# Gated MLP plus spectral filter on one core: h through DRAM as Strassen-Winograd factors, and the down projection in seven products summed in PSUM

## The chip, the cores and the metric

One core of a Trainium2 chip runs the whole kernel. The metric is device time in microseconds of one execution: 1478.47 us, the median of 3 runs (1477.56 to 1479.11). The profile shown below is one further execution, whose span from first to last instruction is 1478.0 us.

## The reference

The input x is 2048 rows of 576 numbers. xn is x with each row brought to mean 0 and variance 1. The output is the sum of x, a spectral filter of xn and a gated MLP of xn:

```python
xn = _layernorm(x, axis=-1)
# A: X = rfft2(xn);  X = X * (w_r + 1j * w_i);  y = irfft2(X)
# B: g = xn @ w_gate; u = xn @ w_up; h = sigmoid(g) * u; y = h @ w_down
return x + _A_ref(xn, A_w_r, A_w_i) + _B_ref(xn, B_w_gate, B_w_up, B_w_down)
```

w_gate and w_up are 576 x 4608, w_down is 4608 x 576, all in float32. F below is the inner width 4608, cut into NF = 36 blocks of 128.

## The kernel before

Each float32 factor is split into a rounded high part (ACT copies it into fp32r) and a low part (DVE subtracts), and a product is three partial products: high by high, high by low, low by high. A product of a 288-row inner dimension takes seven matmuls of 512 columns (`prod`, L554; the last of them holds the 32 rows left over in all three combinations).

The rows of x go in two halves of 1024 ("pairs", p = 0 and 1), each in two chunks of 512. For a half, `X` holds seven transposed and split combinations of its four blocks A11, A12, A21, A22 (two chunks by two halves of D): the left factors of Strassen-Winograd's seven products. `fill` (L343) makes one by transposes on PE, with `prep` and `sums` ahead of it. For each block f of F, `make_w` (L217) loads gate and up columns (`load_raw`, L197) and makes the seven right factors; they go to DRAM (`wsp`, L231) in the first half and come back from there in the second (`get_w`, L243). `unit` (L585) then makes the seven products of one f for one half, 49 matmuls in all, and from their PSUM banks A, B and E the block of h: gate goes through the sigmoid, is multiplied with up (L638), and h is split into hh and hl (L640, L641). The first two blocks of F in each half (`plain`, L566) are done without Strassen-Winograd, with 28 matmuls for each block and chunk.

The down projection is plain. `down` (L643) multiplies, for one tile of 128 rows, two blocks of h (as stationary operand) by two blocks of w_down, split by `make_d` (L250), in two column halves of 288: 12 matmuls into a pair of PSUM banks. DVE then adds the 128 x 576 result to the tile's accumulator in SBUF (L659), which starts as x itself. This follows every second f, for eight tiles, and is issued within the next two units, behind their products 4 and 5.

The spectral part goes in three phases over 16 tiles each, `phase1b` (transform along D and the first stage along S, to DRAM `sc1`), `phase2` (second stage, filter, inverse of that stage, `sc1` to `sc2`), and `phase3` (rest of the inverse, added into the accumulator). Each phase is a generator; the second half of the program steps all active ones once after each product (`beside`, `aside`), and a table with base and rate (L41, L678) says at which step a tile begins. The constants of a phase are loaded in `stage1`, `stage2` and `stage3`. The accumulators of the first half go to DRAM (`spill`) and come back in `phase3`.

Nearly all DMAs are issued by SP's queue. The framework orders the instructions of an engine by its own planning, close to program order; only the first tiles are in an order written by hand (L706). On the chip each engine works in order.

## Time and profile before

| | |
|---|---|
| median of 3 runs | 1478.47 us |
| span of the profiled execution | 1478.0 us |
| PE busy | 1447.0 us, 8232 matmuls and transposes |
| DVE busy | 932.3 us |
| ACT busy | 596.4 us |
| DMA | 307.87 MB, mean 208 GB/s |
| last matmul begun and its chain | PE ends at 1472.7 us, then one add of 0.75 us and the output's DMA |

In the rows of a view, `out<-in` names tiles, x with a number is a count, and the first two numbers behind the bar are the group's busy time in us and the mean of one instruction in ns; behind the second bar stands the idle time just ahead of these instructions, with what ended it. In the rows of time stretches, each engine has its busy us and its count, followed by the granted TensorE clock, the busy share of the 16 DMA engines and GB/s. KB is 1024 bytes, GB/s counts 10^9.

### The profile page before, as it was taken

Reading aid. Unit: us, or ns where it says so; the run is one execution under the profiler, and the core shown is the slowest. Engines: PE = TensorE matmul, PEld = TensorE weight load, DVE = VectorE, ACT = ScalarE, POOL = GpSimd, SP = SyncE. Lnnn points to the kernel's source line nnn. Section 1 sums busy time; section 2 is a strip of 40 time slices with the busy share of each in tenths; the row PEclk is TensorE's granted clock in tenths of the full one; section 3 lists DMA queues with packets and bytes.
Section 4 is the critical chain, followed back from the end, with each engine's and each line's share of the span. In section 5 each row is a group of like instructions: output and inputs, shape, how many; then the busy total and the mean of one; then the engine's idle time right before and its main releaser. Section 6 shows DMA issues by size and latency. Waiting matters only on the chain.

```text
span 1478.0 us, 21446 instructions
## 1 busy us (share of the span) xinstructions
PE 1447.0 (98%) x8232; PEld 1274.7 (86%) x8232; DVE 932.3 (63%) x1608; ACT 596.4 (40%) x1023; POOL 9.7 (1%) x29
## 2 busy tenths in 40 slices
PE   4999999999999999999999999999999999999998
PEld 3788888888888888888888888888888898898897
DVE  4889777777777777766455555546666644555544
ACT  4734434344444434453334344334444433333331
POOL 2000000000000000000000000000000000000000
PEclk9999999999999999999999999999999999999999
DMA  7577666666666666665856455567777576654532
GB/s 210 191 238 244 223 239 239 232 228 225 227 219 216 223 232 238 230 203 195 270 172 212 159 189 170 174 208 243 235 242 247 181 255 223 224 161 163 179 110 65
DMA packets 150487, 307.87 MB, mean 208 GB/s; under 512 B 14064, under 2 KB 77808, under 8 KB 145520
## 3 DMA queue, kind: packets, MB, share of 16 engines
q1 hardware_dynamic: 149072, 304.00, 61.5%
q0 software_dynamic: 384, 1.18, 0.4%
q8 instruction: 65, 1.06, 0.3%
q10 hardware_dynamic: 928, 1.31, 0.2%
q14 instruction: 38, 0.31, 0.1%
HBM read 188.01 MB, written 118.42 MB: 207 GB/s over the span
## 4 chain that ended last, share of the span: by engine, by line
PE 91%; DMA 3%; DVE 3%; ACT 1%; SPq 1%; issue 1%; DVEq 0%; ACTq 0%; POOL 0%; POOLq 0%
PE po L654 30%; PE pB L554 21%; PE pE L554 16%; PE pA L554 15%; PE pe L511 2%; PE pd L401 2%; PE pa L412 1%; PE pc L456 1%; PE py L482 1%; PE pb L440 1%; DMA std<-in_B_w_down 1%; DMA acc<-in_A_x 1%; DMA x<-sc 0%; PE pf L386 0%; PE pz L494 0%
## 5 line engine op out<-in xcount | busy, mean ns | idle before, releaser
L654 PE MATMUL po<-wd,hh 128*128 128x288 f32 x2304 | 401.6, 296 | 2.5 <-DVE acc L659 1.6
L554 PE MATMUL pB<-X,w 128*128 128x512 f32 x1484 | 383.5, 394 | 4.1 <-ACT w L210 3.8
L659 DVE TENSOR_TENSOR acc<-acc,po 128x576 f32<-128x576 f32 x288 | 216.0, 752 | 236.6 <-PE po L654 235.1
L654 PEld LDWEIGHTS po<-wd,hh 128*128 128x128 f32 x2304 | 343.8, 188 | 16.9 <-DVE acc L659 3.6
L554 PEld LDWEIGHTS pB<-X,w 128*128 128x128 f32 x1484 | 271.9, 189 | 55.8 <-ACT w L210 4.2
L554 PE MATMUL pE<-X,w 128*128 128x512 f32 x1064 | 273.5, 392 | 0.0
L554 PE MATMUL pA<-X,w 128*128 128x512 f32 x1008 | 261.2, 394 | 0.6 <-DVE X L356 0.5
L654 PE MATMUL po<-wd,hl 128*128 128x288 f32 x1152 | 246.3, 295 | 0.0
L554 PEld LDWEIGHTS pE<-X,w 128*128 128x128 f32 x1064 | 193.1, 188 | 34.5
L554 PEld LDWEIGHTS pA<-X,w 128*128 128x128 f32 x1008 | 188.2, 190 | 38.1 <-DVE X L356 1.1
L654 PEld LDWEIGHTS po<-wd,hl 128*128 128x128 f32 x1152 | 186.3, 189 | 0.0
L210 ACT ACTIVATE w<-raw 128x768 fp32r<-128x768 f32 (+1 forms) x106 | 100.3, 947 | 108.2 <-PE pE L554 94.6
L618 ACT ACTIVATE g<-pB 128x512 f32<-128x512 f32 x68 | 40.6, 598 | 190.2 <-PE pB L554 190.2
L641 DVE TENSOR_TENSOR hl<-y,hh 128x1024 fp32r<-128x1024 f32 x67 | 82.1, 1225 | 30.0 <-ACT hh L640 29.0
L638 DVE TENSOR_TENSOR y<-y,g 128x1024 f32<-128x1024 f32 x67 | 82.0, 1224 | 3.4
L212 DVE TENSOR_TENSOR w<-raw,w 128x512 fp32r<-128x512 f32 (+1 forms) x106 | 81.9, 772 | 2.6 <-ACT w L210 2.2
L640 ACT ACTIVATE hh<-y 128x1024 fp32r<-128x1024 f32 x67 | 70.7, 1055 | 6.6 <-DVE y L638 6.2
L601 ACT ACTIVATE pB<-pA 128x512 f32<-128x512 f32 x68 | 39.6, 582 | 75.1 <-PE pA L554 75.1
L608 ACT ACTIVATE v<-pB 128x512 f32<-128x512 f32 x68 | 40.6, 597 | 66.0 <-PE pB L554 65.8
L615 DVE TENSOR_TENSOR y<-v,pE 128x512 f32<-128x512 f32 x68 | 46.6, 685 | 32.7 <-ACT v L614 31.6
L637 DVE TENSOR_TENSOR y<-v,pE 128x512 f32<-128x512 f32 x67 | 45.9, 686 | 26.6 <-PE pE L554 26.5
L183 DVE TENSOR_TENSOR al<-pd,ah 64x290 fp32r<-64x290 f32 x64 | 29.3, 458 | 41.0 <-ACT ah L182 40.5
(148 smaller groups left out, 1261.2 us busy)
## 6 DMA issues: line engine op xcount, KB each, us to landing
w<-wsp SPq DMA_DIRECT2D x246, 320.0 KB
wsp<-w SPq DMA_DIRECT2D x34, 2240.0 KB
wdsp<-wd SPq DMA_DIRECT2D x36, 576.0 KB
wd<-wdsp SPq DMA_DIRECT2D x36, 576.0 KB
std<-in_B_w_down SPq DMA_DIRECT2D x36, 288.0 KB
raw<-in_B_w_gate SPq DMA_DIRECT2D x72, 128.0 KB
raw<-in_B_w_up SPq DMA_DIRECT2D x72, 128.0 KB
sc<-x SPq DMA_DIRECT2D x16, 290.0 KB
```

The source lines that it names most:

```text
L210: nc.scalar.activation(o[:, :, :3, :], src, AF.Copy)
L212: nc.vector.tensor_tensor(o[:, :, 3:, :], src[:, :, :KT, :], f32(o[:, :, :KT, :]), op=OP.subtract)
L554: nc.tensor.matmul(bank, w[:, sw, :], X[:, x, sx, :], start=start and j == 0, stop=stop and j == len(STEPS) - 1, skip_group_check=skip)
L608: nc.scalar.activation(v[:, 0], bank["B"], AF.Copy)
L615: nc.vector.tensor_tensor(y[:, 1], v[:, 1], bank["E"], op=OP.add)
L618: nc.scalar.activation(g[:, 1], bank["B"], AF.Sigmoid)
L637: nc.vector.tensor_tensor(y[:, 0], v[:, 0], bank["E"], op=OP.add)
L638: nc.vector.tensor_tensor(y, y, g, op=OP.mult)
L640: ends.extend([first, lambda: nc.scalar.activation(hh, y, AF.Copy), lambda: nc.vector.tensor_tensor(hl, y, f32(hh), op=OP.subtract)])
L641: lambda: nc.vector.tensor_tensor(hl, y, f32(hh), op=OP.subtract)])
L654: nc.tensor.matmul(pd[:, b, :HD], l[:, c, cols], w[:, k, b * HD:(b + 1) * HD], start=g == 0 and l is hh and k == 0, stop=g == G - 1 and l ...
L659: nc.vector.tensor_tensor(a, a, pd[:, :, :HD], op=OP.add)
```

## The change

The program is parted in two. **Part one** makes all of h. X for all 2048 rows (seven factors for each half, in `xps`) stays on chip, so each f's right factors are made once and used for both halves: there is no `wsp` any more. The eight `plain` calls come first, then the units in the order (2,0), (3,0), (2,1), (3,1), then f by f with both halves. A unit's first product is issued inside the unit before (`ahead`). h stays in float32; for each pair of blocks, `export` makes the seven left factors of a second Strassen-Winograd and writes them to DRAM (`ssp`), and `make_t` does the same for w_down with split right factors (`tsp`).

**Part two** computes h times w_down: for each of seven products j and each half p, 18 steps k sum over all of F in four PSUM banks, one for each of four row tiles. A step loads a 128 x 512 block of the left factor (`fetch`), four steps ahead, splits it (`cut`), two steps ahead, and issues 12 matmuls of 288 columns. At k = 17 each bank is added to the accumulators by `evac`. All spectral phases move to part two, with one step of the generators at each of the 252 steps; the accumulators (16 tiles, each loaded from x in one of the first 16 steps) all stay on chip.

Core of the diff (`load_raw`, `make_w`, `fill` and the phases keep their instructions but for names and pools):

```diff
-U1, U2, U3 = (0, 4.1), (72, 4.1), (145, 4.7)
+NPR = NF // 2
...
+    def unit(u, beside, after):
+        f, p = u
+        h = new_h(f, p)
+        g = run.tile([P, 2, CW], F32, tag="g", name=f"g{f}_{p}")
+        B[u, "B"] = bank("bB", f"pB{f}_{p}")
+        B[u, "E"] = bank("bE", f"pE{f}_{p}", 2)
+        bA, bB, bE = (B[u, k] for k in "ABE")
+        nc.scalar.activation(bB, bA, AF.Copy)
+        made(u, "E", "P5", True)
+        beside()
+        made(u, "B", "P6", False)
+        nc.scalar.activation(h[:, 0], bB, AF.Copy)
+        beside()
+        made(u, "A", "P2", False)
+        nc.scalar.activation(g[:, 0], bA, AF.Sigmoid)
+        beside()
+        made(u, "B", "P7", False)
+        nc.scalar.activation(h[:, 1], bB, AF.Copy)
+        nc.vector.tensor_tensor(h[:, 1], h[:, 1], bE, op=OP.add)
+        beside()
+        if after:
+            ahead(after)
+        beside()
+        made(u, "B", "P4", False)
+        nc.scalar.activation(g[:, 1], bB, AF.Sigmoid)
+        beside()
+        made(u, "E", "P3", False)
+        nc.vector.tensor_tensor(h[:, 0], h[:, 0], bE, op=OP.add)
+        nc.vector.tensor_tensor(h, h, g, op=OP.mult)
+        beside()
...
+    def export(k, p):
+        a, b = H[2 * k, p], H[2 * k + 1, p]
+        A11, A21, A12, A22 = a[:, 0], a[:, 1], b[:, 0], b[:, 1]
+        def put(what, src):
+            nc.sync.dma_start(ssp[ORDER.index(what)][p][k], src)
+        put("P1", A11)
+        put("P2", A12)
+        put("P4", A22)
...
+        nc.vector.tensor_tensor(S1, A21, A22, op=OP.add)
+        put("P5", S1)
+        yield
+        nc.vector.tensor_tensor(S2, S1, A11, op=OP.subtract)
+        put("P6", S2)
+        yield
+        nc.vector.tensor_tensor(A21, A11, A21, op=OP.subtract)
+        put("P7", A21)
+        yield
+        nc.vector.tensor_tensor(S4, A12, S2, op=OP.subtract)
+        put("P3", S4)
...
+    ORDER = ("P1", "P2", "P6", "P7", "P4", "P5", "P3")
...
+        elif f >= 3 and p == (1 if f == 3 else 0) and f + 1 < NF:
+            make = make_w(f + 1)
...
+        elif p == 1 and f >= 4 and f + 2 < NF:
+            load_raw(f + 2)
+        if p == 1:
+            sides += [make_t(k) for k in range(NPR) if 4 + k * 5 // 3 == f]
+    finish(*sides)
+    one.close()
+    two = ExitStack()
...
+    def evac(what, p, m, b):
+        v = b[:, :HD]
...
+        if what == "P1":
+            U[p, m] = u = accp.tile([P, HD], F32, name=f"u{p}{m}")
+            nc.scalar.activation(u, v, AF.Copy)
+            add(c11, u)
+        elif what == "P2":
+            add(c11, v)
+        elif what == "P6":
+            add(U[p, m], v)
+            add(c12, U[p, m])
+        elif what == "P7":
+            add(U[p, m], v)
+            add(c21, U[p, m])
+            add(c22, U[p, m])
...
+    seq = [(j, p, k) for j in range(7) for p in range(HALVES) for k in range(NPR)]
+    def fetch(n):
...
+        if p == 0:
+            TT[j, k] = t = ring.tile([P, 2, HD], F32R, tag="t", name=f"tt{j}_{k}", bufs=NPR + 2)
+            nc.sync.dma_start(f32(t).rearrange("p a d -> p (a d)"), tsp[j][k])
+        SF[n] = s = ring.tile([P, CW], F32, tag="sf", name=f"sf{n}", bufs=4)
+        nc.sync.dma_start(s, ssp[j][p][k])
+    def cut(n):
...
+        SP_[n] = s = ring.tile([P, 2, CW], F32R, tag="sp", name=f"sp{n}", bufs=4)
+        split(s[:, 0], s[:, 1], SF[n])
...
+    for (base, rate), phase, n in (((2, 4.5), phase1b, HALVES * TPH), ((80, 4.5), phase2, N2 // 2), ((157, 4.8), phase3, HALVES * TPH)):
+        for t in range(n):
+            begin.setdefault(base + int(t * rate), []).append(lambda t=t, phase=phase: phase(t))
...
+    for n, (j, p, k) in enumerate(seq):
+        if n < HALVES * TPH:
+            load_x(acc[n], n)
+        fetch(n + 4)
+        cut(n + 2)
+        s, t = SP_.pop(n), TT[j, k]
+        for m in range(TPC):
+            if k == 0:
+                M[m] = ps.tile([P, CW], F32, tag=f"m{m}", name=f"m{j}_{p}{m}")
+            o = M[m][:, :HD]
+            for i, (a, b) in enumerate(((0, 0), (0, 1), (1, 0))):
+                nc.tensor.matmul(o, s[:, a, m * P:(m + 1) * P], t[:, b, :], start=k == 0 and i == 0, stop=k == NPR - 1 and i == 2)
+            if k == NPR - 1:
+                evac(ORDER[j], p, m, M[m])
+        active.extend(b() for b in begin.pop(n, []))
+        aside()
-    def down(p, j, m):
...
-            for l, k in ((hh, 0), (hh, 1), (hl, 0)):
-                for b in range(2):
-                    nc.tensor.matmul(pd[:, b, :HD], l[:, c, cols], w[:, k, b * HD:(b + 1) * HD],
-                                     start=g == 0 and l is hh and k == 0, stop=g == G - 1 and l is hl)
```

More of the change, by code (lines that the diff above doesn't have):

```diff
@@ L228, in make_w @@
         yield
[L229 to L232 removed]
+        yield from parts(new_w(f, 2, 2), raw[:, 1:3])
     def make_p(f):
         raw = RAW[f]
[L237 to L240 removed]
@@ new lines, in spectral_glu_kernel, with made, ahead @@
+    B = {}
+    def made(u, b, k, start, stop=True):
+        f, p = u
+        ka, kb = FACTORS[k]
+        prod(B[u, b], weight(f, kb), get_x(p, ka), start, stop, not start)
+    def ahead(u):
+        B[u, "A"] = bank("bA", f"pA{u[0]}_{u[1]}", 2)
+        made(u, "A", "P1", True)
+    def unit(u, beside, after):
+        f, p = u
+        h = new_h(f, p)
[25 more added lines that the diff above has]
+        nc.vector.tensor_tensor(h, h, g, op=OP.mult)
+        beside()
@@ new lines, in spectral_glu_kernel @@
+    ORDER = ("P1", "P2", "P6", "P7", "P4", "P5", "P3")
+    nc.vector.memset(rstd[:, :1], 1.0)
+    nc.scalar.dma_start(idf, con["id"])
+    nc.scalar.dma_start(f32(idr), con["id"])
+    nc.scalar.activation(nmr[:, :1], rstd[:, :1], AF.Sqrt)
+    stage_x(0, 0)
+    load_raw(0)
+    stage_x(0, 1)
+    load_raw(1)
+    stage_x(1, 0)
+    stage_x(1, 1)
+    b0 = bank("bB", "b0")
+    for i in range(CW // P):
+        nc.tensor.matmul(b0[:, i * P:(i + 1) * P], idr, idr, start=i == 0, stop=i == CW // P - 1, skip_group_check=True)
@@ new lines, in spectral_glu_kernel, with tick, finish @@
+    sides = []
+    def tick():
+        sides[:] = [g for g in sides if next(g, sides) is not sides]
+    def finish(*gs):
+        for g in gs:
+            for _ in g:
+                pass
+    queue = {0: [lambda: chunk(0, 1)], 1: [lambda: chunk_stats(1, 0)], 2: [lambda: chunk(1, 0), lambda: chunk_stats(1, 1)],
+             4: [lambda: chunk(1, 1), lambda: export(0, 0)], 5: [lambda: factors(0)]}
+    calls = [(f, p, c) for p in range(HALVES) for c in range(2) for f in range(2)]
+    for n, (f, p, c) in enumerate(calls):
+        sides += [q() for q in queue.get(n, [])]
+        if n == 1:
+            load_raw(2)
+            load_raw(3)
+        plain(f, p, c, tick)
+        if n in (0, 2, 4):
+            finish(*sides)
+            sides.clear()
@@ L364, in phase1b, with landed @@
+    pending = {}
+    def landed(t):
+        pending[t] -= 1
+        if pending[t] == 0:
+            for i, r in enumerate(rows(out, t)):
+                (nc.sync, nc.scalar)[i].dma_start(r, acc[t][i * N1:(i + 1) * N1, :])
     def phase1b(t):
@@ L518, in phase3 @@
         nc.vector.tensor_tensor(up, up, pe[:, 0, 1:HD], op=OP.add)
-        if t < TPP:
-            for i, r in enumerate(rows(out, t)):
-                nc.sync.dma_start(r, a[i * N1:(i + 1) * N1, :])
+        landed(t)
     def stage1():
```

697 lines of the change are left out of this document (296 added, 401 removed).

## The prediction

> **What bounds the kernel now.** I read the page first, for which engine fills the span and what the work is made of, then the chain that ended last.
>
> ```profile
> span 1478.0 us, 21446 instructions
> PE 1447.0 (98%) x8232; PEld 1274.7 (86%) x8232; DVE 932.3 (63%) x1608; ACT 596.4 (40%) x1023; POOL 9.7 (1%) x29
> PE 91%; DMA 3%; DVE 3%; ACT 1%; SPq 1%; issue 1%; DVEq 0%; ACTq 0%; POOL 0%; POOLq 0%
> L654 PE MATMUL po<-wd,hh 128*128 128x288 f32 x2304 | 401.6, 296 | 2.5 <-DVE acc L659 1.6
> L554 PE MATMUL pB<-X,w 128*128 128x512 f32 x1484 | 383.5, 394 | 4.1 <-ACT w L210 3.8
> L554 PE MATMUL pE<-X,w 128*128 128x512 f32 x1064 | 273.5, 392 | 0.0
> L554 PE MATMUL pA<-X,w 128*128 128x512 f32 x1008 | 261.2, 394 | 0.6 <-DVE X L356 0.5
> L654 PE MATMUL po<-wd,hl 128*128 128x288 f32 x1152 | 246.3, 295 | 0.0
> ```
>
> PE is the bound, and almost nothing is ahead of its matmuls. The work is 3556 products of 512 columns and 3456 of 288; the rest is the spectral part and transposes. The mean of one (296 ns) is a latency, since matmuls overlap. What one costs is its interval, from the chain and from PE's timeline:
>
> ```profile
> 304.94 3.18 PE po L654 x24
> 314.37 1.75 PE L554 MATMUL pA<-X,w 128*128 128x512 f32 x7
> 315.95 1.75 PE L554 MATMUL pE<-X,w 128*128 128x512 f32 x7
> ```
>
> 3.18 / 24 = 0.1325 us for 288 columns; seven of 512 take 315.95 - 314.37 = 1.58 us, 0.226 each. So 3556 x 0.226 = 804 us are gate and up, 3456 x 0.1325 = 458 us are down. Since the chain follows PE, a matmul removed is worth its interval as long as something feeds the others; the rest of this asks for that.
>
> **The change part by part.** *Matmuls.* Gate and up stay as they are: 8 plain calls of 28 and 68 units of 49 are again 3556. Down becomes 7 products x 2 halves x 18 steps x 4 tiles x 3 = 3024 instead of 3456. Each still has a stationary block of h and 288 moving columns, so the interval is kept: 432 x 0.1325 = **-57.2 us**. Without any other effect: 1478.0 - 57.2 = 1420.8. The profiled span is 0.5 us below the median of the runs, so I take it as the run's time.
>
> *Part one.* Without the 12-matmul blocks there are only products of 1.58 us, and the question is whether DVE keeps pace:
>
> ```profile
> 100.00:700.00 600.00, 599.02 (x3349) 531.85 (x3349) 447.33 (x742) 249.61 (x366) 0.00 (x0) 1.00 0.65 226
> L583 DVE TENSOR_TENSOR hl<-y,hh 128x512 fp32r<-128x512 f32 x6 | 4.1, 689 | 2.0 <-ACT hh L582 2.0
> L582 ACT ACTIVATE hh<-y 128x512 fp32r<-128x512 f32 x5 | 3.1, 629 | 4.7 <-DVE y L581 4.7
> L334 DVE TENSOR_TENSOR xa<-xa 128x288 f32<-128x288 f32 x4 | 1.6, 451 | 0.0
> ```
>
> DVE was 75% busy there, and PE had no hole. An f took 49 x 0.226 + 48 x 0.1325 = 17.4 us, so DVE spent 13.0 us on it. To that come, for an f of two units in 98 x 0.226 = 22.1 us: the second unit's adds (four times 128x512, 2.8 us), `export` (eight adds for two f, 2.8) and half of a `make_t` (eleven of 128x288, 2.5). That is 21.1 us even with nothing taken off for the accumulator adds and the split of h, which leave: it fits. I put part one's steady state at 0, hidden under PE; what it costs if a wait breaks that cover is the rival on late weights below.
>
> *The start.* It now prepares four chunks and both halves' factors beside plain calls and the first units; before, the second half's came later. Rows of PE's timeline, and the clock after the last hole:
>
> ```profile
> 12.72 0.69 PE L351 MATMUL px_A<-idf,xa 128*128 128x128 f32 x2 [7.35 <-ACT xa L329]
> 21.17 0.69 PE L351 MATMUL px_A<-idf,xa 128*128 128x128 f32 x2 [5.74 <-ACT xa L329]
> 37.64 1.70 PE L554 MATMUL pB<-X,w 128*128 128x512 f32 x3 [3.76 <-ACT w L210]
> 36.00:42.00 6.00, 3.88 (x14) 2.66 (x15) 5.24 (x20) 5.75 (x10) 0.00 (x0) 0.57 0.57 191
> ```
>
> The holes of 7.35, 5.74 and 3.76 us are waits on x and the first weights. w_down's load and split leave this place, but the second chunk's x now goes behind eight weight loads on SP instead of POOL. In those 6 us DVE is 5.24 busy: it sets the pace of preparing, and twice as much of it now lies under about 50 us of plain calls. Between -5 (w_down gone) and +12 (about two holes more), I take **+2**.
>
> *The seam.* Between the parts stands a DRAM round trip and memory handed from X to the new buffers. The nearest row is the one in the middle of the spectral part, on the chain:
>
> ```profile
> 968.63 4.34 DMA sc<-x
> 972.99 7.11 DMA x<-sc
> ```
>
> If the first step had to wait for its write and read, 4.34 + 7.11 = 11.5 us. But product P1's first pieces were written by the first export, hundreds of us earlier, and x0's buffers are free one unit (11 us) before the end; then it costs a fill of the pipe. After a hole of 3.76 us the clock was 0.57 for 6 us, 2.6 us lost, so 14 is the upper bound and 0 the lower. I take **+4**. The tail (PE's end, a DVE add, the output's DMA) is as before: 0.
>
> *Feeding part two.* This is the dear one. A step is 12 x 0.1325 = 1.59 us of PE, and in a first half (p = 0) it loads 256 KB of h's factor and 288 KB of w_down's. With that travel the spectral transfers:
>
> ```profile
> cf<-c_cf SPq DMA_DIRECT2D x1, 1450.0 KB
> acc<-in_A_x SPq DMA_DIRECT2D x24, 144.0 KB
> am<-c_am SPq DMA_DIRECT2D x16, 256.0 KB
> xb<-in_A_x SPq DMA_DIRECT2D x32, 144.0 KB
> x<-sc SPq DMA_DIRECT2D x16, 290.0 KB
> sc<-u SPq DMA_DIRECT2D x16, 290.0 KB
> wr<-in_A_w_r SPq DMA_DIRECT2D x32, 144.5 KB
> 805.00:810.00 5.00, 5.00 (x30) 4.24 (x28) 1.37 (x3) 2.48 (x7) 0.00 (x0) 1.00 1.03 405
> 850.00:855.00 5.00, 4.92 (x24) 3.78 (x24) 2.88 (x5) 2.85 (x6) 0.00 (x0) 1.00 1.00 364
> 325.00:330.00 5.00, 5.00 (x34) 4.70 (x34) 2.00 (x3) 0.60 (x1) 0.00 (x0) 1.00 1.01 420
> 1180.00:1200.00 20.00, 20.00 (x112) 17.71 (x112) 8.89 (x11) 6.34 (x10) 0.00 (x0) 1.00 0.87 308
> ```
>
> With the DMA engines full (share 1.00 to 1.03), 5 us moved 364, 405 and 420 GB/s. I take 380, between the first two, in which weights were read in rows of 2.5 KB, nearest to the new 2 and 2.3 KB. Where PE's own step is longer than its bytes, nothing is lost. Steps 0 to 15 also load an accumulator (2 x 144 KB): from step 2 with a tile of `phase1b` every 4.5 steps (256 + 288 + 290 KB; 20 matmuls of 290 columns and 6 transposes, about 3.1 us of PE), a step moves 1017 KB, 2.74 us, against 1.59 + 0.68 = 2.27 us: 14 x 0.47 = 6.6. Steps 0 and 1 lack the spectral cover and cf's 1450 KB go in step 1: 2 x 0.65 + 3.9 = 5.2. Steps 80 to 151 carry `phase2`: 290 + 4 x 144.5 + 290 KB for each tile (wr and wi, two loads each), 257 KB per step, against 12 matmuls, 0.35 us. In a first half that is 801 KB, 2.16 us, against 1.94; 36 steps of these are first halves: 7.8. The constants of `phase3`, as large as cf, fall into another: 3.9. Elsewhere PE's step is longer. Sum **+23 us**; the same sum gives 11 at 420, 29 at 364 and 66 at 308 GB/s.
>
> The Trainium skill ("DMA: Bandwidth & Descriptors", Specifications) puts HBM at about 358 GB/s for one core; by that the term would be 31 us. The rows at 405 and 420 GB/s lie above it, as the Trainium skill's "HBM Reference", Access, says of a core that streams alone.
>
> *Splitting h seven times* moves to part two: ACT 0.63 and DVE 0.69 us per step by the rows of L582 and L583, under 1.59 us of PE. With the spectral work DVE is the fuller one, in `phase2`:
>
> ```profile
> L183 DVE TENSOR_TENSOR x2l<-x,x2h 128x580 fp32r<-128x580 f32 x16 | 12.1, 755 | 3.3 <-ACT x2h L182 3.3
> L447 DVE TENSOR_TENSOR z<-wr,pb 128x512 f32<-128x512 f32 (+2 forms) x48 | 16.7, 352 | 20.6 <-ACT sw L443 16.9 <-DMA w<-wsp 3.4
> L449 DVE TENSOR_TENSOR z<-z,t 128x578 f32<-128x578 f32 x16 | 12.1, 753 | 0.0
> L412 PEld LDWEIGHTS pa<-ah,am 128*128 128x128 f32 x64 | 11.7, 188 | 7.4 <-ACT ah L182 6.5
> L456 PEld LDWEIGHTS pc<-zh,bmt 128*128 128x128 f32 x64 | 11.2, 188 | 5.5 <-ACT zh L182 5.3
> ```
>
> A tile of it has two splits of 0.755, an add of 0.753 and twice three multiplies of 0.352: 4.4 us per 4.5 steps. That is 0.98 + 0.69 = 1.67 us per step, under 1.94: DVE is at 86% and not last.
>
> *Ends of products.* Each tile has one bank, so the next product's first matmul on it waits for the add out of it; cover is nine matmuls, 1.2 us. With one 0.451 us add per tile (0.4 us of PE) it just holds. P6 queues two and P7 three adds per tile: the last of four banks is read after 3 x 0.9 + 0.45 = 3.2 and 3 x 1.35 + 0.45 = 4.5 us, where PE needs it 2.4 us after the first: 0.8 + 2.1, for two halves 5.8; a `cut` of 0.69 in front at each of 14 ends would make it 15.5. Bounds 0 and 16, I take **+5**.
>
> *Spectral chains.* Before, PE's weight loads waited 7.4 and 5.5 us for ACT at the two worst places. The chains keep their steps, now one per 1.59 us or more: 0, from -10 (hidden where the feed is slower anyway) to +13 (these two waits twice as long).
>
> Sum: 1478.0 - 57.2 + 2 + 4 + 23 + 5 = **1455 us**.
>
> **The rivals.** *The feed does not sustain its rate (slower).* 405 and 364 GB/s are five full us; the best 20 us quoted have 308, at a share of 0.87. In part two SP issues every load in order, and a store of `phase1b` or `phase2` that waits for ACT holds back the next `fetch`, which is ahead by only four steps (two before `cut`). If such holes hold the feed to 308, the term is 66 and the time 1478.0 - 57.2 + 11 + 66 = 1498. It decides from 46 us of feed on, about 328 GB/s. For it: at steps 2 to 15 PE's own pace of 2.27 us would ask for 459 GB/s, more than any row. Against it: other steps ask far less, and most of part two is not bound by the feed.
>
> *All hidden.* The scheduler runs loads early enough and start and seam cost nothing: 1421. For it: PE went without holes at 226 GB/s. Against it: the bytes of steps 0 to 15.
>
> *The lower row of reads holds throughout*: with full engines, but 364 GB/s, the feed is 29 us and the time 1461. The row at 364 and, over 20 us, 308 speak for it, 405 against. The Trainium skill's limit of HBM above is the rule for this case; by it the time is 1463.
>
> *Weights come late in part one (no change).* `make_w` for f + 2 starts in the very unit behind whose predecessor `load_raw` is issued; before, it had a whole unit between.
>
> ```profile
> 324.63 1.24 SPq L204 DMA_DIRECT2D raw<-in_B_w_gate  x1
> 333.46 0.55 SPq L205 DMA_DIRECT2D raw<-in_B_w_up  x1
> ```
>
> Its eight loads took 334.01 - 324.63 = 9.4 us to issue. ACT, waiting for them, would hold the copies out of bank B behind it, for which PE has 1.58 us of cover. If each odd f (16 of them behind seven writes of `export`) lost 1.4 us: 23 us, 1478.
>
> **How the numbers follow.** Forecast 0.45, all hidden 0.15, the lower row 0.10, late weights 0.08, slow feed 0.22. A measurement of this kernel tells 0.2%, 3 us, from no change, so the first three are faster (0.70), late weights the same (0.08), slow feed slower (0.22). The forecast alone spans 1436 to 1472: feed 11 to 29, seam and ends at their bounds. The range 1426 to 1494 takes in all but half of the hidden case and the worse half of the slow feed.
>
> **What would show it.** Right: 3024 matmuls of 288 columns at 0.1325 us between starts; part two begun about 855 us into the span (804 us of products and the start's holes and transposes); a DMA share near 1 in the first 50 us of part two and in first halves under `phase2`, with PE's idle there put down to the split or its load; short holes at the ends of P6 and P7. Wrong: holes in part one behind ACT's `w<-raw` (late weights), a DMA share well under 1 where PE waits (the queue, not the bytes), DVE over 95% in part two, or a clock under 1.00 in the rows of part two, which would add PE time that I have not counted.

## The result, and the profile after

The changed kernel takes **1522.43 us** (median of 4 runs, 1514.74 to 1524.78) against 1478.79 us for the kernel before in the same session: a ratio of 1.0289 (95% interval 1.0263 to 1.0314). It is slower by about 44 us. The forecast was 1455 us in a range of 1426 to 1494.

First the page of the changed kernel: its span, the busy time of the engines, the granted TensorE clock and the DMA share in 40 slices of 38 us, and the down projection's group.

```profile
span 1519.5 us, 22486 instructions
PE 1437.7 (95%) x7800; PEld 1242.0 (82%) x7800; DVE 971.3 (64%) x1808; ACT 702.7 (46%) x1292; POOL 1.7 (0%) x20
PEclk9999999999999999999999987999999999999999
DMA  7234445545545555455554379788888888895954
L904 PE MATMUL m<-tt,sp 128*128 128x288 f32 x3024 | 453.8, 302 | 32.4 <-ACT sp L135 27.3
```

The 432 matmuls are gone (7800 for 8232), as the diff says. PE's busy share fell from 98% to 95%. The last row shows one place: 32.4 us of idle time stand ahead of the new matmuls, 27.3 of them ended by the rounding copy of h's factors. The DMA row jumps from mostly 4 and 5 tenths to 7 and more at the 24th slice, where part two begins.

For the rest I measured the time from each matmul's start to the next one's, form by form. Below, an *interval* is the usual value of that, and a *loss* is what single ones take beyond it. By that measure part two begins at 888.8 us, not at 855, and four things changed.

| | forecast, us | in the profile, us |
|---|---|---|
| 508 products of seven matmuls, each 1.587 us before | 0 | 508 x 0.053 = 27 |
| losses in part one behind its first 60 us | 0 | 20 |
| losses in the first 60 us (29.6 before) | 31.6 | 18.6 |
| losses in part two (35.8 outside the start before, kept, plus 4 + 23 + 5) | 68 | 30 + 35 + 26 + 7 = 98 |

The four terms of the last row are, by place: the first 60 us of part two 30, up to 300 us of it 35, from there to 410 us (the filter phase) 26, the rest 7. The differences are +27, +20, -13 and +30: 64 us, and 1455 + 64 = 1519, where the span is 1519.5. So the sum closes, and the question is what stands behind each. (The 27 us are the change of the usual value times a count; what it costs in time is asked below.)

The first difference can be read from two neighbouring rows of PE's timeline, the second from a stretch of part one; columns as in the rows of the prediction.

```profile
330.85 1.79 PE L349 MATMUL pA<-X0A,w 128*128 128x512 f32 x7
332.48 1.79 PE L349 MATMUL pB<-X0S,w 128*128 128x512 f32 x7
```

```profile
100.00:700.00 600.00, 593.01 (x2542) 473.62 (x2541) 397.53 (x644) 258.31 (x441) 0.00 (x0) 1.00 0.52 176
```

Seven matmuls take 332.48 - 330.85 = 1.63 us where they took 1.58, at a granted clock of 1.00, so it isn't the clock. And PE, which had one hole of a microsecond in these 600 us, now lacks seven, although DVE is *less* busy than before (397.53 for 447.33 us) and ACT is at 43%. A busy share does not tell this; the waits do. These are ScalarE's longest, by line and releaser (us in total, times, longest), in part one:

```profile
ACT tP L452 <- DMA ts<-tP: 128.5, 88, 5.7
ACT g L405 <- PE pB L349: 102.8, 48, 2.9
ACT h L392 <- PE pB L349: 75.9, 50, 3.7
```

The second and third are harmless: ACT is early and waits for a product. The first is new. L452 makes the rounded part of one w_down factor; its tile has one buffer, so it waits until the store of the factor before has landed. What that does shows in the timeline:

```profile
736.74 0.41 SPq L455 DMA_DIRECT2D ts<-tP  x1
...
738.83 1.81 PE L349 MATMUL pA<-X1A,w 128*128 128x512 f32 x7
...
741.38 0.44 ACT L452 ACTIVATE tP<-wd 128x288 fp32r<-128x288 f32 x1 [5.70 <-DMA ts<-tP]
...
741.73 0.58 ACT L392 ACTIVATE h<-pB 128x512 f32<-128x512 f32 x1
...
742.36 3.19 PE L349 MATMUL pB<-X1S,w 128*128 128x512 f32 x7 [1.72 <-ACT h L392]
```

ACT stands still for 5.70 us on a copy that nobody needs soon. Behind it in its queue stands the copy of h out of bank B, which PE's next product on that bank needs (there is one such bank), and PE waits 1.72 us. This is the usual case: followed back one by one in the trace, PE's holes of part one that end with a copy of ACT's sum to 13.4 us, and 9.3 of them stand right behind a copy of L452 that had just waited for a landing. Another 1.5 us stand behind L452 waiting for something else, 1.8 us behind the weights' copies (L203) waiting for VectorE.

In part two the first 60 us are the worst: three stretches of 20 us.

```profile
900.00:920.00 20.00, 8.12 (x30) 6.92 (x30) 3.02 (x6) 2.23 (x6) 0.10 (x1) 0.50 1.03 256
920.00:940.00 20.00, 16.80 (x92) 14.94 (x93) 8.80 (x16) 7.42 (x17) 0.10 (x1) 0.84 1.01 265
940.00:960.00 20.00, 16.12 (x96) 14.21 (x95) 6.85 (x13) 6.21 (x14) 0.10 (x1) 0.90 1.00 276
```

The DMA engines are full (1.00 to 1.03), yet they move 256 to 276 GB/s and not the 364 to 420 of the full stretches before. So it is bytes, as I forecast, but at another rate. The order of the transfers adds to it:

```profile
898.77 3.00 SPq L145 DMA_DIRECT2D acc<-in_A_x  x4
...
901.25 3.25 PE L904 MATMUL m<-tt,sp 128*128 128x288 f32 x12 [3.98 <-ACT sp L135]
...
907.06 0.33 SPq L865 DMA_DIRECT2D sf<-ss  x1
...
909.81 1.17 SPq L145 DMA_DIRECT2D acc<-in_A_x  x2
...
913.79 0.63 ACT L135 ACTIVATE sp<-sf 128x512 fp32r<-128x512 f32 x1 [12.59 <-DMA sf<-ss]
...
914.47 3.49 PE L904 MATMUL m<-tt,sp 128*128 128x288 f32 x12 [9.97 <-ACT sp L135]
```

The accumulators' loads, wanted some 15 steps later, stand in front of the factor that PE wants now. PE idles 3.98 and 9.97 us, and the clock is 0.50 in the first of the three stretches (0.75 from 899 to 960 us, and 0.93 in the filter phase, from 1195 to 1300 us).

PE's waits in part two do not all belong to the feed:

```profile
PE m L904 <- ACT sp L135: 27.3, 14, 10.0
PE pa L691 <- DVE al L136: 5.8, 7, 1.7
PE pc L735 <- ACT zh L135: 3.6, 5, 1.2
PE m L904 <- DVE sp L136: 2.7, 4, 1.1
PE m L904 <- DVE u L827: 2.2, 1, 2.2
```

The first and the fourth row, 30.0 us, are waits for the split of h's factors. The waits inside the spectral chains (`pa`, `pc` and smaller groups of `pd`, `pf` and `pz`) sum to 16.3 us, most of them between 949 and 1189 us, where the split accounts for only 3.1 us. In the same view of the second half of the kernel before (from 739 us on), PE's waits of all kinds sum to 1.8 us. The last row is the end of a product. The rest of the 98 us is in no wait of this view: intervals that are longer than usual, those at the lower clock among them.

### The profile page after: what moved, and what is told of

It is laid out like the page before. It is cut to its first block, busy times and chain, and to the rows that moved or that the text cites. A ratio compares the mean times of both kernels' runs of the same rounds, so it can differ in the third digit from the quotient of the medians.

```text
span 1519.5 us, 22486 instructions
## 1 busy us (share of the span) xinstructions
PE 1437.7 (95%) x7800; PEld 1242.0 (82%) x7800; DVE 971.3 (64%) x1808; ACT 702.7 (46%) x1292; POOL 1.7 (0%) x20
## 5 line engine op out<-in xcount | busy, mean ns | idle before, releaser
L904 PE MATMUL m<-tt,sp 128*128 128x288 f32 x3024 | 453.8, 302 | 32.4 <-ACT sp L135 27.3
L904 PEld LDWEIGHTS m<-tt,sp 128*128 128x128 f32 x3024 | 424.6, 193 | 38.3 <-ACT sp L135 31.0
L136 DVE TENSOR_TENSOR sp<-sf,sp 128x512 fp32r<-128x512 f32 x252 | 172.3, 689 | 124.8 <-ACT sp L135 122.3
L135 ACT ACTIVATE sp<-sf 128x512 fp32r<-128x512 f32 x252 | 157.3, 629 | 144.1 <-PE m L904 71.5
L349 PE MATMUL pA<-X0A,w 128*128 128x512 f32 (+1 forms) x518 | 137.3, 402 | 2.2 <-DVE w L205 1.4
L349 PE MATMUL pA<-X1A,w 128*128 128x512 f32 (+1 forms) x518 | 133.0, 396 | 0.0
L349 PE MATMUL pB<-X1S,w 128*128 128x512 f32 (+1 forms) x476 | 124.0, 400 | 3.2 <-ACT h L392 3.2
L349 PE MATMUL pE<-X0S,w 128*128 128x512 f32 (+1 forms) x490 | 126.4, 397 | 0.0
L203 ACT ACTIVATE w<-raw 128x768 fp32r<-128x768 f32 (+2 forms) x108 | 100.2, 931 | 56.2 <-DVE raw L229 27.1
L349 PE MATMUL pE<-X1S,w 128*128 128x512 f32 (+1 forms) x490 | 125.9, 396 | 0.0
L349 PE MATMUL pB<-X0S,w 128*128 128x512 f32 (+1 forms) x476 | 122.7, 397 | 0.6 <-ACT h L392 0.5
L452 ACT ACTIVATE tP<-wd 128x288 fp32r<-128x288 f32 x126 | 55.9, 443 | 139.1 <-DMA ts<-tP 128.5
```

The lines of the kernel that those rows point to most:

```text
L135: nc.scalar.activation(hi, src, AF.Copy)
L136: nc.vector.tensor_tensor(lo, src, f32(hi), op=OP.subtract)
L203: nc.scalar.activation(o[:, :, :3, :], src, AF.Copy)
L349: nc.tensor.matmul(b, w[:n, sw, :], xx[:n, sx, :], start=start and j == 0, stop=stop and j == len(STEPS) - 1, skip_group_check=skip)
L452: nc.scalar.activation(t[:, 0], src, AF.Copy)
L904: nc.tensor.matmul(o, s[:, a, m * P:(m + 1) * P], t[:, b, :], start=k == 0 and i == 0, stop=k == NPR - 1 and i == 2)
```

## The experiments

Each time stands beside the kernel before on the same chip (1476.9 to 1477.6 us in these sessions); the changed kernel's ratio is 1.0289. Where intervals of two ratios overlap, I read only the trace, not the difference. When I planned the first runs my theory was that the lengthened interval came from the last step of each product, which uses 96 rows instead of 128, that the waits on the tP store made the holes of part one, and that part two lost to bytes; the rivals were a held SP queue and the place of the weights in memory.

### The matmuls' interval

**Last step on 128 rows** (e1), and **the kernel before with 96 rows** (e2):

```diff
-            n = KR if sx == KT else P
+            n = P            # the unused rows of X are set to zero
```

> The changed kernel with all seven steps of a gate/up product on 128 rows again (unused rows set to zero once). Theory of the narrow step: the 96-row matmul, new in this change, lengthens the interval of the 512-column matmuls from 227 to about 234 ns; undone, intervals return to 227 ns, part one ends about 25 us earlier and the time falls by about 25 us (1497). Rival (the longer interval comes from what part one does beside PE: other places in SBUF, other traffic): intervals stay at 232 to 235 ns and the time is unchanged within 4 us.

> The kernel before with one thing of the change: the last step of each product on 96 rows instead of 128. Theory of the narrow step: intervals of the 512-column matmuls go from 227 to about 234 ns and the time rises by about 25 us (1503). Rival: intervals stay at 227 ns, time within 4 us of 1478.

e1: 1512.79 us, ratio 1.0239 (1.0209 to 1.027); seven matmuls still took 1.638 us. e2: 1485.55 us, ratio 1.0054 (1.0039 to 1.0069); 1.613 us. In the kernel before the narrow step does cost something, 8 us where I expected 25, but putting it right in the changed one does not bring 1.587 back. There is a second cause. By the sizes of the tiles ahead of them, the changed kernel's weight tiles do not begin at a multiple of 128 bytes in a partition's memory (the first two lie 96 bytes past one); before, all did. No trace shows addresses; the runs that move the tiles have to tell.

**Weights moved to multiples of 128 bytes** (e8), and **the kernel before with them moved off by 32** (e9):

```diff
+    nc.gpsimd.memset(run.tile([P, 24], F32, name="pad"), 0.0)   # last in its pool
```

This is e8's edit. e9 puts a pad of 32 bytes ahead of the weight tiles of the kernel before, and one of 96 behind them.

> The changed kernel with one pad of 96 bytes at the end of part one's right pool, so that the stationary blocks of gate and up begin at multiples of 128 bytes in SBUF, as in the kernel before, and not 96 behind one. Theory of the shifted weights: this place, not the narrow step, makes the interval of the 512-column matmuls 234 instead of 227 ns; it returns to near 227 (231 where the narrow step shows), and the time falls by 17 to 25 us. Rival (something else in part one): the interval stays at 232 to 235 ns, time within 4 us of the changed kernel.

> The kernel before with a pad of 32 bytes ahead of its weight tiles and of 96 behind them, so that the stationary blocks of gate and up begin 32 bytes behind a multiple of 128; all else keeps its place modulo 128. Theory of the shifted weights: interval 234 ns instead of 227 in all products, time up by 20 to 25 us. Rival: interval 227 ns, time unchanged within 4 us.

e8: 1517.26 us, 1.0268 (1.0239 to 1.0297), so no gain in time; products 6 and 4 still took 1.640 us, the others 1.596 to 1.618. e9: 1486.84 us, 1.0063 (1.0046 to 1.0079); its timeline:

```profile
331.58 1.79 PE L554 MATMUL pE<-X,w 128*128 128x512 f32 x7
333.21 1.79 PE L554 MATMUL pA<-X,w 128*128 128x512 f32 x7
```

1.63 us, with nothing changed in the kernel before but the place of its weights. The time tells less than the interval: 0.045 us more for each of 508 products would be 23 us, and the kernel took 9.7 us longer. **Both edits together** (e14):

> The changed kernel with both edits at once: the last step of each product on 128 rows (unused rows zero), and the weights moved so that each begins at a multiple of 128 bytes. Each alone left the seven 512-column matmuls of a product at 1638 and 1617 to 1640 ns, against 1587 in the kernel before. Theory of two causes that hide one another: 1585 to 1592 ns for seven, median interval 227 ns, part two begins at 862 to 870 us, time 1494 to 1503 us. Rival (a third cause, such as which bank or which factor stands where): intervals stay at 231 ns or more, time 1510 us or more.

e14: 1514.15 us, 1.0263 (1.0227 to 1.03). Five of a unit's seven products take 1.587 to 1.593 us, products 6 and 4 take 1.621, and the median interval is 227 ns as before: the two causes hide one another. Products 6 and 4 are the two that read the third weight tile, `new_w(f, 2)`; product 7, on the same bank B but from the second tile, takes 1.587 us. So the bank is not what slows them. In the program the small tiles `st` and `rs` lie between the third weight tile and the others; e15 and e16 below move them elsewhere, and there all seven products are alike. That the pad left the third tile off a multiple of 128 is the reading that fits; no run moved this tile alone. But the time hardly moved. Part two begins at 882.7 us instead of 888.8, because the losses of part one rose from 20 to 38 us:

```profile
100.00:700.00 600.00, 587.51 (x2558) 474.07 (x2557) 400.11 (x648) 261.05 (x444) 1.04 (x2) 1.00 0.51 176
```

2558 matmuls in 600 us for 2542 before the edits, with 12.5 us idle for 7.0. PE was not what set the pace of part one. On time my expectation (1494 to 1503) missed, and the holes became the first question.

### The holes of part one

**The stores of the factors issued by GpSimd** (e3), to take SP's queue out of the wait:

```diff
-            nc.sync.dma_start(tsp[ORDER.index(what)][k], ...)
+            nc.gpsimd.dma_start(tsp[ORDER.index(what)][k], ...)
```

> The changed kernel with the stores of w_down's factors in part one issued by POOL instead of SP. ACT waited 128 us in sum for the landing of the one buffer's store before it could fill it again, with the copies out of bank B behind it. Theory (these waits make part one's holes, some 17 us): the waits shrink by more than half, as the store no longer queues behind SP's weight loads, and the time falls by 8 to 15 us. Rival (the wait is the landing itself, not SP's queue, or the holes have another cause): ACT's waits stay above 100 us and the time changes by less than 4 us.

1562.2 us, 1.0586 (1.0564 to 1.0609): wrong in sign. The stores landed later (among those that a copy waited for, a median of 3.8 us behind VectorE's rest, for 2.8), and the wait grew from 128.5 us to this:

```profile
ACT tP L452 <- DMA ts<-tP: 209.0, 86, 5.5
```

The losses of part one went from 20 to 66 us, and 43 us of PE's holes now stand right behind such a wait, for 9.3. A longer wait on this line costs PE time; that much is shown.

**The factor's two parts in two tiles** (e10):

```diff
-            t = run.tile([P, 2, HD], F32R, tag="tt", ...)
+            hi = run.tile([P, HD], F32R, tag="th", ...)   # own store, one step earlier
+            lo = run.tile([P, HD], F32R, tag="tl", ...)
```

> The changed kernel, with the two parts of each w_down factor (its rounded value and its rest) in two tiles of one buffer each instead of one tile for both, each part written to DRAM on its own, the rounded value's store one step earlier. In the changed kernel ScalarE waited 128.5 us in 88 waits for the landing of the store before, with the copies of h queued behind it, and TensorE lost 20 us in the steady state of part one. Single-buffer theory (this wait costs TensorE the time): the waits fall to under 70 us, the holes to about 10 us, part two begins at 875 to 882 us instead of 888.8, time 1508 to 1515 us. Rival (the holes come from the length of ScalarE's and VectorE's own work, the wait only shows it): waits fall but the holes stay at 17 to 22 us, time 1519 to 1524 us.

1534.01 us, 1.0379 (1.0359 to 1.04), also the wrong way. The wait moved to another releaser and grew:

```profile
ACT thP L453 <- DVE tlP L457: 158.8, 76, 4.8
...
ACT thP L453 <- DMA ts<-thP: 43.2, 25, 5.4
```

The rounded part's buffer comes free only when VectorE has made the rest from it, and VectorE in its turn waits for the rest's buffer. Losses of part one: 30 us.

**Two buffers for the factor** (e15, on aligned weights), room made by writing one sum of `export` in place; and **with 128 rows too** (e16):

```diff
-            t = run.tile([P, 2, HD], F32R, tag="tt", name=f"t{what}{k}")
+            t = run.tile([P, 2, HD], F32R, tag="tt", name=f"t{what}{k}", bufs=2)
```

> The changed kernel with weights at multiples of 128 bytes (1617 to 1640 ns for seven matmuls, 1517.3 us measured before) and two buffers instead of one for the w_down factors of part one; the room comes from writing one sum of h's factors in place. It stands against that aligned kernel. Single-buffer theory: ScalarE's waits for the store's landing fall from over 100 us to under 20 us, the holes of part one's steady state from 29 to under 12 us, part two begins about 867 to 872 us instead of 887, time 1497 to 1504 us. Rival (ScalarE's and VectorE's own work sets the pace of part one): waits move to other lines, part two begins at 882 us or later, time 1512 us or more.

> As the run with two factor buffers, with the last step of each product on 128 rows as well. Without the two buffers these faster matmuls (1593 ns for seven on the banks A and E, 1620 to 1629 on B) raised the holes of part one from 20 to 38 us and moved its end by only 6 us. Single-buffer theory: holes under 15 us, part two begins at 846 to 856 us, time 1475 to 1487 us. Rival (ScalarE and VectorE set the pace): holes stay at 30 us or more, part two begins at 875 us or later, time 1505 us or more.

e15: 1521.73 us, 1.0295 (1.027 to 1.0319), with 1.613 us for seven matmuls, what e2's narrow step alone gave. e16: 1520.48 us, 1.0294 (1.0274 to 1.0315), although all seven-matmul products in it take 1.587 us, as before the change:

```profile
331.41 1.75 PE L351 MATMUL pE<-X0S,w 128*128 128x512 f32 x7
333.00 1.75 PE L351 MATMUL pB<-X0S,w 128*128 128x512 f32 x7
```

```profile
100.00:700.00 600.00, 576.88 (x2514) 464.70 (x2513) 409.94 (x680) 264.52 (x463) 1.04 (x2) 1.00 0.55 189
```

PE is idle for 23 of these 600 us. Waits for the landing stay at 93 us in 58 times in e15 and 99 us in 61 times in e16, the losses at 29 us (e15) and 39 us (e16), so a second buffer is no cure as the framework used it. But these runs are no clean test of the wait, since the order changed too: in e16 the copies come several in a row (a median of 2.3 us from one to the next, for 5.0 in e14), and the last is made at 603 us, for 828. Of the 30.6 us of e16's holes that end with a copy of ACT's, 19.6 us still stand right behind a wait for a landing. What the change of order shows by itself is more telling. These are two stretches of e16, the second behind the last of the copies:

```profile
300.00:500.00 200.00, 191.47 (x827) 153.28 (x825) 135.55 (x232) 88.29 (x158) 0.00 (x0) 1.00 0.59 203
700.00:860.00 160.00, 160.00 (x708) 132.53 (x707) 94.12 (x135) 60.96 (x93) 0.00 (x0) 1.00 0.32 113
```

PE lacks 8.5 us in the first and nothing in the second. The holes end with the work on w_down's factors.

**The factors' arithmetic taken out** (e19, on 128 rows and aligned weights): loads and stores stay, a constant tile is stored.

```diff
-            nc.scalar.activation(t[:, 0], src, AF.Copy)
-            nc.vector.tensor_tensor(t[:, 1], src, f32(t[:, 0]), op=OP.subtract)
-            nc.sync.dma_start(tsp[ORDER.index(what)][k], f32(t)...)
+            nc.sync.dma_start(tsp[ORDER.index(what)][k], f32(H["t"])...)   # H["t"] set once
```

> The changed kernel with aligned weights and 128-row last steps (1514.2 us, holes of part one 38 us, part two at 882.7 us), without the arithmetic on w_down's factors: ScalarE's 126 rounding copies and VectorE's 126 differences and its sums are left out, a constant tile is written to DRAM in their place, so loads and stores of w_down stay. Queue theory (these copies stand in ScalarE's queue ahead of the copies of h and g that TensorE's next product needs, and wait there for a store's landing): holes fall to under 10 us, part two begins at 848 to 856 us, time 1480 to 1488 us. Rival (the bank of the third sum, which has one buffer, makes the holes by itself): holes stay at 25 us or more, part two at 872 us or later, time 1503 us or more.

1489.78 us, 1.0083 (1.0062 to 1.0103). The losses of part one fall to 9.9 us, and part two begins at 855.2 us: the point that I had forecast.

```profile
100.00:700.00 600.00, 600.00 (x2650) 494.09 (x2649) 351.77 (x506) 231.86 (x357) 1.04 (x2) 1.00 0.52 178
```

PE has no hole in 600 us, with the same bank B and nearly the same bytes as e14 (178 GB/s for 176). More of them travel early: from 100 to 300 us it is 297 GB/s, and PE is busy for 200.00 of these 200 us. So the bank alone makes no holes, nor do the transfers; the factor work in the queues of ScalarE and VectorE does. That e14's and e19's medians lie 24 us apart is its price, in this version. Taking the wait and the work out one at a time would tell how they share it; e19 takes out both.

**All factor work on GpSimd** (e20, on e16, with two easings of part two):

```diff
-            nc.scalar.activation(t[:, 0], src, AF.Copy)
+            nc.gpsimd.tensor_copy(t[:, 0], src)
...
-            nc.vector.tensor_tensor(t[:, 1], src, f32(t[:, 0]), op=OP.subtract)
+            nc.gpsimd.tensor_tensor(t[:, 1], src, f32(t[:, 0]), op=OP.subtract)
```

> The changed kernel with aligned weights, 128-row last steps, two factor buffers, all work on w_down's factors (loads, copies, differences, stores) on GpSimd and its queue, and in part two factors fetched eight ahead and accumulators loaded every second step. Queue theory: part one's holes fall to under 12 us, part two begins at 850 to 858 us, its first 300 us lose 50 to 58 us instead of 65, time 1468 to 1480 us, about the kernel before. Rival (GpSimd is too slow for 126 pairs in part one, or takes VectorE's access to SBUF): holes of 25 us or more, or factors late for part two, time 1500 us or more.

1520.54 us, 1.0286 (1.0246 to 1.0326). The losses of part one stay at 38 us, with other releasers: PE's longest wait is now for VectorE (10.9 us), and ScalarE's copies still end 11.8 us of its waits. GpSimd's factor work is done at 535 us; from 700 to 860 us PE is busy throughout, as in e16. These are two of VectorE's groups from 100 to 500 us, first without GpSimd's work (e19), then with it (e20); the last pair of numbers before the second bar is busy us and mean ns.

```profile
L410 DVE TENSOR_TENSOR h<-h,pE 128x512 f32<-128x512 f32 x36 | 24.8, 688 | 87.6 <-PE pE L351 87.4
...
L431 DVE TENSOR_TENSOR s<-s,h 128x512 f32<-128x512 f32 x17 | 11.7, 689 | 0.3
```

```profile
L410 DVE TENSOR_TENSOR h<-h,pE 128x512 f32<-128x512 f32 x33 | 22.7, 688 | 57.6 <-PE pE L351 57.3
...
L431 DVE TENSOR_TENSOR s<-s,h 128x512 f32<-128x512 f32 x16 | 17.6, 1102 | 0.3
```

The add that takes one operand from PSUM keeps its 688 ns; the same add with both operands in SBUF goes from 689 to 1102 ns. So this moves the trouble to VectorE and settles nothing about a version with free queues on all sides, which I did not run.

### The feed of part two

**Stores and loads of the spectral phases on GpSimd's queue** (e4), for the rival that a held SP queue starves the factors:

```diff
-        nc.sync.dma_start(x2, ...)
+        nc.gpsimd.dma_start(x2, ...)     # also sc1, sc2 stores, w_r and w_i
```

> The changed kernel with four kinds of spectral transfers in part two (stores to sc1 and sc2, loads of x2 and of wr and wi) issued by POOL instead of SP; the bytes are the same. Theory of the held queue: SP, waiting for ACT's copy to store it, holds back the loads of h behind it; without that the 27 us that PE lost between 1200 and 1300 us fall below 10, time down 15 to 25 us. Theory of the bytes: the feed is short of GB/s, not of order; time changes by less than 5 us.

1516.68 us, 1.0266 (1.0249 to 1.0283), overlapping the changed kernel's interval. In the filter phase the losses fell from 26 to 20 us, from 60 to 300 us they rose from 35 to 44. What these four kinds of transfers hold up in SP's queue is not the main loss.

**Factors fetched eight steps ahead** (e5):

```diff
-        fetch(n + 4)
+        fetch(n + 8)     # sf bufs 4 to 8, t bufs NPR + 2 to NPR + 6
```

> The changed kernel with part two's loads issued eight steps ahead instead of four (eight buffers for h's blocks, four more for w_down's). Theory of the order (PE waits since SP is held by spectral stores or by a free buffer, while the DMA engines have room): PE's waits between 960 and 1300 us, some 50 us more than the products need, fall by more than half and the time by 20 to 35 us. Theory of the bytes (the engines are full there): they fall by less than a quarter, time down by under 8 us, and the first 60 us of part two stay as they are in both.

1511.01 us, 1.0224 (1.0208 to 1.024), about 10 us better by the ratios. The first 20 us of part two gained (93 matmuls and transposes for 30), the first 60 us as a whole lost 31 as before: depth shifts the bytes there and does not remove them. Behind it the losses fell from 35 to 30 us. In e20, which also loads the accumulators every second step instead of every step, the first 60 us lost 23 us; no run has this edit alone.

**The two halves of each x load on two queues** (e6):

```diff
-            (eng or nc.sync).dma_start(dst[i * N1:(i + 1) * N1], r)
+            (nc.sync, nc.gpsimd)[i].dma_start(dst[i * N1:(i + 1) * N1], r)
```

> The changed kernel with the two 64-row loads of each tile of x (accumulators and phase1b's tiles in part two) on two queues, SP and POOL, instead of one behind the other on SP. Theory of the half transfer: a load that fills 64 of 128 partitions goes at some 200 GB/s, and two halves side by side reach over 300, so the first 60 us of part two lose 10 to 20 us less and the time falls by that. Rival (rows of x are slow to read because they lie 73 KB apart in DRAM): packets of 2304 bytes still take 150 to 190 ns there, time unchanged within 5 us.

1527.28 us, 1.0341 (1.0312 to 1.037), no gain; on SP's queue the packets of 2304 bytes still took 151 ns on average from 899 to 960 us. The x rows come as two transfers to 64 partitions each, and these packets take long: 149 ns on average from 899 to 960 us in the changed kernel. Is it the half set of partitions, or the 73 KB from row to row?

**128 contiguous rows in one transfer** (e11) and **in two of 64** (e12):

```diff
-        for i, r in enumerate(rows(x, t)):
-            (eng or nc.sync).dma_start(dst[i * N1:(i + 1) * N1], r)
+        (eng or nc.sync).dma_start(dst, x.rearrange("b s d -> (b s) d")[t * P:(t + 1) * P])
```

> The changed kernel, with each load of x rows in part two (the sixteen accumulators and the norm's rows) as one transfer of 128 contiguous rows instead of two of 64 rows that lie 32 rows apart; it adds and normalizes the wrong rows, same number of bytes. In the changed kernel the packets of these loads took 144 to 190 ns beside 93 ns of the other loads. Transfer-shape theory: packets of 90 to 110 ns, the first 60 us of part two lose 14 to 20 us instead of 30, time 1508 to 1514 us. Rival (the queues are full of bytes whatever their shape): the first 60 us still lose 27 us or more, time 1519 us or more.

> As the run with 128 contiguous rows, but in two transfers of 64 contiguous rows to the two halves of the partitions (wrong rows again, same bytes). If the half set of partitions makes the packets long: packets of 140 ns or more, time as the changed kernel, 1517 us or more. If the rows' distance in DRAM does: packets under 110 ns, time as the run with 128 rows, 1508 to 1514 us.

e11: 1508.8 us, 1.021 (1.019 to 1.023), about 12 us better by the ratios, packets of 101 ns. e12: 1522.15 us, 1.0293 (1.0269 to 1.0317), packets of 147 ns. The same stretches as above, for e11:

```profile
900.00:920.00 20.00, 15.25 (x86) 14.27 (x87) 7.61 (x15) 6.06 (x13) 0.10 (x1) 0.71 1.04 394
920.00:940.00 20.00, 17.18 (x107) 15.36 (x105) 9.63 (x20) 8.36 (x19) 0.20 (x2) 0.91 0.91 291
940.00:960.00 20.00, 19.11 (x132) 17.66 (x132) 14.16 (x29) 11.80 (x28) 0.20 (x2) 1.00 0.78 270
```

and the first for e12:

```profile
900.00:920.00 20.00, 11.07 (x51) 9.83 (x52) 4.27 (x8) 2.95 (x7) 0.10 (x1) 0.60 1.01 272
```

With full engines 394 GB/s on 128 partitions, 272 on twice 64: the half set of partitions is the cause, and rows that lie together don't help it. The Trainium skill ("SBUF — State Buffer", "Can I just issue two DMAs to hit both halves?") states that two transfers to two halves do not add up, since only one transfer over all 128 partitions reaches all ports of the memory. e6, e11 and e12 agree with it.

**One transfer of 128 partitions, rows as they must be** (e17):

```diff
+        b, s2 = divmod(2 * t, N2)
+        nc.sync.dma_start(dst, x[b].rearrange("(s1 s2) d -> s2 s1 d", s2=N2)[s2:s2 + 2])
```

> The changed kernel with each load of x rows in part two as one transfer of 128 partitions instead of two of 64, the rows still 32 rows apart in DRAM. The run with contiguous rows on 128 partitions gave 1508.8 us and 101 ns packets, contiguous rows on 64 partitions 1522.2 us and 147 ns. If the half set of partitions is all of it: packets 95 to 115 ns, the first 60 us of part two lose 20 to 23 us instead of 30, time 1506 to 1512 us. If the rows' distance counts too: packets 130 ns or more, time 1516 us or more.

1676.89 us, 1.1356 (1.1339 to 1.1373): far off. The packets are short now (112 ns, though with the engines far from full). But look at a stretch in which little else travels:

```profile
918.00:922.00 4.00, 0.00 (x0) 0.00 (x0) 0.00 (x0) 0.00 (x0) 0.00 (x0) 0.50 0.13 49
```

A DMA share of 0.13 is 2.1 of 16 engines. The source's slowest dimension is the pair of rows, of size 2. The Trainium skill ("DMA: Bandwidth & Descriptors", "Why a DMA increments its semaphore by 16 and not by 1") says that a transfer runs on the largest number of engines up to 16 that divides the slowest dimension of both sides. For a 2 that is two engines; the trace agrees.

**All edits together** (e18), which contained this transfer, and the same form for w_r and w_i:

> The changed kernel with all edits that answer to a loss: last step on 128 rows, weights at multiples of 128 bytes, two factor buffers, x rows and the filter's w_r and w_i as one transfer of 128 partitions, factors of part two fetched eight ahead. If the losses add: part two begins at 846 to 856 us, its first 300 us lose 40 to 50 us instead of 65, time 1448 to 1465 us, so below the kernel before. Rival (the loss moves to the bytes that part two needs): its first 300 us still lose 60 us, time 1470 to 1485 us, no better than before.

1792.32 us, 1.2151 (1.2122 to 1.218). Part two began at 884.7 us, and the two-engine transfers took the rest, so it says nothing on whether the cures add. No version that I ran beats the kernel before.

## Why the prediction was wrong, step by step

*Matmuls, -57.2 us.* Right in count, and the interval of the 288-column ones held (302 ns of latency for 296, and 0.132 us between starts). "Gate and up stay as they are" was not right: the same 3556 matmuls went from 227 to 234 ns, 27 us by the count of the table. Two things that I did not look for in the diff did it, the 96-row step and where the weights begin in memory (e2, e9, e14, e16). In time they cost less: in the kernel before e2 and e9 cost 8 and 9.7 us, and e14 and e16 show that taking the change away gains only 5 to 6 us at the end of part one, since the holes grow instead.

*Part one's steady state at 0, "hidden under PE".* **This is the first step that failed.** Part two began at 888.8 us instead of 855. I compared DVE's busy time with PE's for one f, found 21.1 under 22.1 us, and called it covered. As a sum that was safe (DVE was busy for 397.53 of 600 us, 66%, where my sum had 95%), but a sum of busy times is not the test: in ScalarE's order, a rounding copy that waits for a store's landing stands ahead of the copy out of bank B that PE needs. ScalarE, at 43%, was the engine, which I had not examined at all for this place. The holes come with the work on w_down's factors (e16, e19), and more than half of those that end with a copy of ACT's stand right behind a wait for a landing (9.3 of 13.4 us; 43 us when e3 lengthened the wait). How the wait and the copies themselves share the rest is not shown. The rival that I named there, late weights, did not decide: ScalarE's waits for their loads sum to under 10 us. e19 puts the price at 24 us on a version with faster matmuls; with the work out, part two begins at 855.2 us. That it is the forecast point to the microsecond is luck: by its trace, e19's start is some 12 us better than forecast, and its remaining losses (9.9 us) and two slower products of each unit about make up for it. What the holes cost at the slower interval of the changed kernel itself I have only from its trace: 20 us.

*The start, +2.* It was -11 (18.6 us of losses for 29.6), below my lower bound of -5. With w_down's work gone from there, preparing twice the chunks beside plain calls fits. No run tested this by itself.

*The feed, +23.* **This is the second step that failed, in its size**: the losses of part two were 98 us, where all terms of the forecast together had 68. The mechanism was right (full DMA engines in the first steps and under the filter phase, PE waiting for the split or its load, 30.0 us of waits), the rate was not. I took 380 GB/s from rows in which 128 partitions were filled; x rows go to 64, and the stretch ran at 256 to 276, below 308, the lowest rate that I priced. Of the losses, e11 returns about 12 us and e5 about 10. The rival "slow feed, held SP queue" had the sign, and its 1498 us for the wrong half of its reason: e4 shows that the held queue matters little. It also left part one alone. The sign that I had named for time not counted, a clock under 1.00 in part two, was there as well (0.75 in the first stretch, 0.93 in the filter phase).

*Spectral chains, 0.* PE's waits for them were 16.3 us in part two, above the 13 that I had as the upper bound. I read what a weight load waited for in the kernel before, and took the longer step to be cover enough.

*Seam and ends, +4 and +5.* The seam is not separable from the feed in the trace: the 3.98 and 9.97 us ahead of the first matmuls are waits for factors behind the accumulators' loads. Of the ends, the trace shows one wait of 2.2 us, behind the adds of U (L827). With the bounds given there (feed 11 to 29, seam 0 to 14, ends 0 to 16) the forecast alone spans 1434 to 1482, not 1436 to 1472.

Mending one of the two was not enough in any run: e19, without the first, stays at 1489.78 us, and e11, with a part of the second returned, at 1508.8.

*What is still open:* how much of part one's holes a version would lose whose copies need not wait, with all else in place; and how the 98 us of part two divide beyond the waits above. A version that loads x once instead of twice was not tried.

## What to carry to other kernels

Ask of every instruction that waits for a DMA what stands behind it in its engine's queue, even when the engine is half idle; a sum of busy times under the bound's does not answer that. Before a transfer's bytes are priced, see how many partitions it fills and over how many DMA engines it is divided, and take the rate from a row of the same shape. When a part that looks like the bound is made faster and the time stays, as in e14 and e16, it wasn't the bound: look for who ends the new holes.

## What the runs showed of the hardware that I had not expected

- Seven matmuls of 512 columns with a 128 x 128 fp32r weight block take 1.587 us in the kernel before, and 1.632 us when a pad moves its weight tiles by 32 bytes (e9); a last step of 96 rows among steps of 128 makes it 1.613 us (e2). The two do not add: 1.640 us in the changed kernel, which has both.
- A stretch of 20 us with all DMA engines busy moved 272 GB/s with the 2304-byte rows of x going to 64 partitions at a time, and 394 with them going to 128 (e12, e11).
- A transfer whose slowest dimension is 2 ran on 2.1 of 16 DMA engines (e17).
- VectorE's add of two SBUF operands went from 689 to 1102 ns beside GpSimd's work; with one operand in PSUM it stayed at 688 ns (e20).
